# A gated linear recurrence and a gated MLP on one core: a smaller first and last unit, a different order of loads, and two decays summed on TensorE

## The chip, the cores and the metric

The kernel runs on one core of one Trainium2 chip. The metric is the device time of one execution in microseconds (us). Most executions of one kernel agree within about half a per cent. An execution that is over 1.5% above the fastest of the same kernel is called slow.

"Span" is the time from the first to the last instruction in the trace. It is about 2 us shorter than the device time of the same run.

## The reference, cut to what matters

```python
# q, k, v, a_re, a_im: (4, 8, 768, 48) float32: batch, heads, time, head size
mag = np.sqrt(a_re * a_re + a_im * a_im)
scale = np.minimum(mag, 0.999) / (mag + 1e-06)
a = a_re * scale, a_im * scale                 # complex gate, magnitude at most 0.999
for t in range(S):                             # state S: 48 x 48 for each batch and head
    S_re, S_im = a[t] * S + k[t] v[t]^T        # (complex product; k v^T is real)
    y[t] = q[t] @ S_re
x = y as (3072 tokens, 384)                    # heads side by side
g = x @ w_gate                                 # 384 x 1536
val = x @ w_val                                # 384 x 1536
ffn_out = (gelu(g) * val) @ w_out              # 1536 x 384
out = x + sigmoid(x @ w_res) * ffn_out
```

## The kernel before

The time axis is cut into 12 groups of 256 tokens (g = 0 to 11, each of C = 2 chunks of 128 tokens). Three groups make one batch element, so groups 0, 3, 6 and 9 begin with an empty state. Every other group needs the *decay* of its boundary, called M: the exponential of the log magnitudes summed over the last chunk of the group before and the first chunk of this one. The state that is carried over is multiplied by it. (The kernel before has it as a product of three factors: the last chunk of the group before, the first token of this one, and the rest of this first chunk.)

Two groups make a *unit* of 512 tokens. The program alternates two phases for each unit. `phase_x(u)` holds the output matmuls of unit u-1 (`op`), the second half of the attention of unit u, the cumulative sums of the gates (`csl`, `cst`) and the ScalarE work on the gates (Ln, Exp, Arctan, Sin). `phase_y(u)` holds the gate matmuls of unit u (`gp`, `vp`, with Gelu on ScalarE), the products q·E and k/E on VectorE, and the first half of the attention of unit u+1. All loads of `ar`, `ai` (gates), `q` and `k` are issued by SP (SyncE); those of `v` and of the weights, which also convert to bf16, by POOL (GpSimd).

The decay is a row of numbers along the free dimension, while the state wants it along the partitions. The kernel before turns it by writing the row to DRAM and reading it back, twice for each group:

```python
def turn(nm, g, srcs):
    n = len(srcs)
    md = dr.tile([n, DM], FP, tag="d" + nm, name="d" + nm)       # in DRAM
    for i, src in enumerate(srcs):
        nc.gpsimd.dma_start(out=md[i:i + 1, :], in_=src)
    m = mp.tile([128, n, H], FP, tag=nm, name=nm)
    for u in range(2):
        nc.gpsimd.dma_start(out=m[u * D:(u + 1) * D].rearrange("p r h -> p (r h)"),
                            in_=md.rearrange("r (h d) -> d (r h)", h=H))
    T[nm, g] = m

def decay0(g):                                                   # first bounce
    turn("m1", g, [T["lm", g][0:1, 0:DM]])
def decay1(g):                                                   # ScalarE
    m = T["m1", g]
    act(out=m[0:DD], in_=m[0:DD], func=AF.Exp)
def decay2(g):                                                   # second bounce
    turn("m2", g, [T["E", g - 1][127:128, DM:W], T["Ei", g][0:1, 0:DM]])
def decay3(g):                                                   # two VectorE products
    m = T["m2", g]
    M = mp.tile([128, H], FP, tag="M", name="M")
    nc.vector.tensor_tensor(out=M[0:DD], in0=m[0:DD, 0], in1=m[0:DD, 1], op=OP.mult)
    nc.vector.tensor_tensor(out=M[0:DD], in0=M[0:DD], in1=T["m1", g][0:DD, 0], op=OP.mult)
    T["M", g] = M
```

The exponential of `decay1` opens `phase_x` on ScalarE. Each engine works through its own list in order:

```python
def phase_x(u):
    g1, g2 = gs(u + 1), gs(u + 2)
    # ... cut: the lists of steps
    weave((0.0, 0.12, csls), (0.05, 0.5, zip_steps([p1(g) for g in g2])), (0.01, 0.01, dec1), (0.12, 0.45, exs),
          (0.46, 0.46, dec), (0.2, 0.65, cst), (0.7, 0.95, atn + sin), (0.95, 0.95, dec3),
          (0.0, 0.8, att), (0.1, 1.0, ops))
def phase_y(u):
    # ... cut
    weave((0.0, 1.0, gv), (0.0, 0.4, pr), (0.3, 0.95, att_steps(u + 1, 0)))

for g in gs(0) + gs(1):
    load_a(g)
for g in gs(0):
    load_q(g)                               # q, k and v
after_landing(T["k", 0], load_w_in)         # w_gate, w_val, w_res
for u in range(-1, NU + 1):
    phase_x(u)
    for g in gs(u + 3):
        load_a(g)
    if u == -1:
        for g in gs(1):
            load_q(g)
        after_landing(T["k", 2], load_w_out)
    phase_y(u)
    for g in gs(u + 3):
        load_q(g)
```

(The two numbers ahead of each list are the shares of the phase over which `weave` spreads its steps.)

Of the kernel before, what the change touches and what calls it, by code (L numbers as in the profile page):

```python
# [9 lines left out]
FP = mybir.dt.float32  # L10
BF = mybir.dt.bfloat16
AF = mybir.ActivationFunctionType
OP = mybir.AluOpType
# [15 lines left out]
def kernel(  # L29
# [23 lines left out]
    NG = B * NS  # L53
    NU = NG // 2
    MAGIC = 12582912.0
# [20 lines left out]
    ones2pi = singles.tile([128, 128], FP, name="ones2pi")  # L76
    nc.vector.memset(ones2pi, I2PI)
    mask4 = singles.tile([128, 4, 128], BF, name="mask4")
    for jm in range(4):
# [47 lines left out]
    def load_a(g):  # L127
        for nm, src in (("ar", a_re), ("ai", a_im)):
            t = lda.tile([128, C, H, D], FP, tag=nm, name=nm)
            for c in range(C):  # L130
                nc.sync.dma_start(out=t[:, c], in_=rows(src, g, c))
            T[nm, g] = t

    def load_q(g):
        for nm, src in (("q", q), ("k", k)):
            t = ldq.tile([128, C, H, D], FP, tag=nm, name=nm)
            for c in range(C):
                nc.sync.dma_start(out=t[:, c], in_=rows(src, g, c))
            T[nm, g] = t
        t = ldv.tile([128, C, H, D], BF, tag="v", name="v")  # L140
        for c in range(C):
            nc.gpsimd.dma_start(out=t[:, c], in_=rows(v, g, c))  # L142
        T["v", g] = t

    def load_w_in():

        FQ = FF // 4
        for i in range(4):
            for w, src in ((wg, moe_w_gate), (wv, moe_w_val)):
                nc.gpsimd.dma_start(out=w[:, :, i * FQ:(i + 1) * FQ],  # L150
                                    in_=src[:, i * FQ:(i + 1) * FQ].rearrange("(i p) m -> p i m", p=128))
        nc.gpsimd.dma_start(out=wr, in_=moe_w_res.rearrange("(i p) m -> p i m", p=128))
# [117 lines left out]
    def decay3(g):  # L270
# [4 lines left out]
        T["M", g] = M  # L275

    def products(g):
        def x0():
# [110 lines left out]
    def xt_step(u, jj):  # L389
        if jj == 0:  # L390
            T["xT", u] = xtp.tile([128, KD, 512], BF, tag="xT", name="xT")
        tpx = psM.tile([128, DM], BF, tag="mm", padded_shape=[128, 1024], name="tpx")
        x = T["x", u * 4 + jj]
        for f in range(KD):
# [8 lines left out]
    def gv_step(u, ffi):  # L403
        xT = T["xT", u]
        if ffi == 0:
            T["h2", u] = hb.tile([128, KF, 512], BF, tag="h2", name="h2")
        h2 = T["h2", u]
        gp = psM.tile([128, 512], FP, tag="mm", name="gp")
        for fi in range(KD):
            nc.tensor.matmul(out=gp, lhsT=wg[:, fi, ffi * 128:(ffi + 1) * 128], rhs=xT[:, fi, :],  # L410
                             start=(fi == 0), stop=(fi == KD - 1))
        vp = psM.tile([128, 512], FP, tag="mm", name="vp")
        for fi in range(KD):
# [16 lines left out]
    def op_step(u, jj):  # L430
# [6 lines left out]
        nc.vector.scalar_tensor_tensor(out=ot, in0=T["sg", u][:, jj], scalar=1.0, in1=ps, op0=OP.add, op1=OP.mult)  # L437
        nc.vector.tensor_tensor(out=ot, in0=ot, in1=T["x", u * 4 + jj], op=OP.add)
        t0 = (u * 4 + jj) * 128
        nc.sync.dma_start(out=out[t0:t0 + 128, :], in_=ot)  # L440
# [7 lines left out]
    def gs(u):  # L448
        return [2 * u, 2 * u + 1] if 0 <= u < NU else []

# [6 lines left out]
    def att_steps(u, half):  # L457

        steps = []
        for g in gs(u)[half:half + 1]:  # L460
            for c in range(C):
                steps += attention(g, c)
                if c > 0:
                    steps.insert(-1, call(xt_step, u, half * C + c - 1))
            steps.append(call(xt_step, u, half * C + C - 1))
        return steps

    def phase_x(u):

        pend = []  # L470
        g1, g2 = gs(u + 1), gs(u + 2)
        d1 = [g for g in g1 if g % NS > 0]
        d2 = [g for g in g2 if g % NS > 0]
        ops = [call(op_step, u - 1, jj) for jj in range(4)] if 0 <= u - 1 < NU else []
        att = att_steps(u, 1)
# [10 lines left out]
        def p1(g):  # L486
            return p1_steps(g) + ([call(decay0, g)] if g % NS > 0 else [])
        csls = [call(csl, g, c) for g in g1 for c in range(C)]
# [8 lines left out]
        if u < 0:  # L497

            for f in [st for g in g1 for st in p1(g)] + csls + exs + dec + zip_steps([p1(g) for g in g2]) + dec1:
                f()  # L500
            for f in atn[:1] + [call(p1_arctan, g) for g in g1] + cst + sin + atn[1:] + dec3:
                f()
            return
# [3 lines left out]
    def phase_y(u):  # L507

        gv = []
        if 0 <= u < NU:  # L510
            table("gelu_and_others")()
            gv = [call(gv_step, u, f) for f in range(KF)]
            gv = gv[:8] + [call(rp_step, u, 0), call(rp_step, u, 1)] + gv[8:] + [call(rp_step, u, 2), call(rp_step, u, 3)]
        pr = [st for g in gs(u + 1) for st in products(g)]
# [4 lines left out]
    for g in gs(0):  # L519
        load_q(g)  # L520
    after_landing(T["k", 0], load_w_in)
    for u in range(-1, NU + 1):
        phase_x(u)
        for g in gs(u + 3):
            load_a(g)
        if u == -1:
            for g in gs(1):
                load_q(g)
            after_landing(T["k", 2], load_w_out)
        phase_y(u)  # L530
        for g in gs(u + 3):
            load_q(g)


# [28 lines left out]
```

## Time and profile before

| | before |
|---|---|
| device time, median | 344.3 us (342.71 to 344.8, 4 runs) |
| span of the profiled run | 341.4 us |
| first transposes of the attention (`tp`) | 48.2 us |
| first gate matmul (`gp`) | 89.85 us |
| start of the first phase that runs at the steady pace | 120.0 us |
| a steady cycle of two phases, 512 tokens | 44.4 to 47.2 us |
| last gate phase, which no other work fills | 312.0 to 329.4 us |
| last outputs | 8.0 us |

First the span in 40 equal slices of 8.5 us, for the kernel before. A digit is the busy share in tenths. PEclk is the granted clock of TensorE, in tenths of full speed.

```profile
PE   0330544298689979899897999779999989999995
...
PEclk9996585559699999999999999999999999999999
DMA  9999999999999999527422620021000210002002
```

(The trace records the clock from 24.8 us on only; the nines before that stand for no record.) TensorE (PE) is nearly full from the twelfth slice to the end. In the first eight slices it is busy 2.6 tenths in the mean, and the next three look better than they are, since the clock is at half in the ninth and at 0.6 in the eleventh. The DMA engines are busy in every slice up to the sixteenth. So there are two limits, one after the other: the start-up, and then TensorE.

The view of windows of the kernel before says the same with numbers. Its columns are the stretch, its length, then the busy time (and number of instructions) of PE, PEld, DVE, ACT and POOL, the granted clock, the DMA share and GB/s.

```profile
100.00:130.00 30.00, 27.83 (x233) 16.93 (x235) 21.91 (x38) 22.25 (x43) 6.57 (x9) 1.00 1.12 152
...
280.00:310.00 30.00, 29.70 (x293) 18.79 (x296) 23.04 (x42) 16.81 (x31) 0.00 (x0) 1.00 0.04 15
```

The chain of waits, followed back from the last instruction, shows what the start-up is made of. These are some of its pieces in the kernel before: start, length, engine and transfer.

```profile
21.80 6.91 DMA dm_219<-ar
...
31.32 5.61 DMA m_247<-dm_244
...
44.80 13.88 DMA dm_266<-ar
...
59.62 4.62 DMA m_268<-dm_266
```

`dm` is a row on its way to DRAM and `m` the same row on its way back. A row of 384 floats is 1.5 KB. In these pieces it takes 7 to 14 us on the way out and about 5 us on the way back. The timeline of the kernel before shows who waits for it, and what the gate loads cost at the very beginning. Columns: start, length, engine, line, operation, tiles, and in brackets the idle time before it and what ended that.

```profile
10.36 4.65 SPq L131 DMA_DIRECT2D ar<-in_a_re_dram  x2
...
15.06 4.57 SPq L131 DMA_DIRECT2D ai<-in_a_im_dram  x2
...
64.32 0.21 ACT L119 ACTIVATE m_268<-m_268 96x8 f32<-96x8 f32 x1 [8.90 <-DMA m_268<-dm_266]
...
89.85 0.58 PE L410 MATMUL gp<-xT,wg 128*128 128x512 bf16 x1 [2.12 <-DVE xT L401]
```

ScalarE waits 8.9 us for a bounced row, in a phase in which TensorE waits for ScalarE. SP spends 4.6 us on a pair of gate loads of 192 KB each, because the v loads that GpSimd started are under way at the same time. That a second issuing engine gives no second path is what the Trainium skill says (DMA: Bandwidth & Descriptors, section "Issuing engines are not separate DMA queues"): all transfers interleave on the same 16 engines.

### The profile page before, as it was taken

How to read it: one execution, taken by the hardware profiler on the slowest of the kernel's cores; microseconds unless marked ns; L12 is line 12 of the kernel's file. 1: busy time of each engine (PE TensorE's matmuls, PEld its weight loads, DVE VectorE, ACT ScalarE, POOL GpSimd, SP SyncE). 2: the span in 40 equal slices, each digit the busy share in tenths (PEclk: the TensorE clock that was granted, in tenths of full speed). 3: DMA queues.
4: the chain of work that ended last, by engine and by line, in shares of the span. 5: the costliest groups of instructions: out<-in, count | busy, mean ns of one | idle time of the engine just before them, and what ended most of it. 6: DMA issues, size and time to landing. Idle time of an engine off the chain costs nothing.

```text
span 341.4 us, 5552 instructions
## 1 busy us (share of the span) xinstructions
PE 267.3 (78%) x2054; PEld 160.6 (47%) x2080; DVE 245.4 (72%) x440; ACT 203.0 (59%) x338; POOL 67.1 (20%) x104
## 2 busy tenths in 40 slices
PE   0330544298689979899897999779999989999995
PEld 0110224275256545465554566445665556565452
DVE  1322696249999649999389998499994799855443
ACT  3365434349665696756896656977568275662530
POOL 9423710050522224102232000150001300000000
PEclk9996585559699999999999999999999999999999
DMA  9999999999999999527422620021000210002002
GB/s 139 136 139 175 176 184 196 175 170 171 155 167 162 169 133 172 109 46 72 25 63 54 118 46 2 2 48 47 3 2 1 50 46 2 0 2 92 2 1 92
DMA packets 135258, 30.25 MB, mean 89 GB/s; under 512 B 127168, under 2 KB 135232, under 8 KB 135232
## 3 DMA queue, kind: packets, MB, share of 16 engines
q1 hardware_dynamic: 103296, 23.60, 40.6%
q0 software_dynamic: 31936, 6.31, 21.9%
q8 instruction: 16, 0.26, 0.3%
q14 instruction: 10, 0.08, 0.1%
HBM read 31.33 MB, written 4.76 MB: 106 GB/s over the span
## 4 chain that ended last, share of the span: by engine, by line
PE 47%; DMA 18%; DVE 15%; ACT 9%; issue 7%; POOL 3%; ACTq 0%; DVEq 0%; POOLq 0%
PE vp L414 12%; PE gp L410 11%; PE op L434 6%; DMA dm_266<-ar 4%; DMA v<-in_v_dram 4%; PE tp L320 3%; PE at L327 3%; PE tp L317 3%; PE rp L426 3%; DMA dm_663<-Ei 2%; ACT L445 2%; DVE fg L237 2%; DVE r L234 2%; DMA dm_219<-ar 2%; ACT CS L119 2%
## 5 line engine op out<-in xcount | busy, mean ns | idle before, releaser
L410 PE MATMUL gp<-xT,wg 128*128 128x512 bf16 x196 | 61.5, 382 | 7.6 <-DVE xT L401 4.6
L414 PE MATMUL vp<-xT,wv 128*128 128x512 bf16 x210 | 60.3, 382 | 0.3
L322 ACT COPY qk<-tp 96x512 bf16<-96x512 bf16 x48 | 27.9, 581 | 28.3 <-PE tp L320 15.1
L180 DVE TENSOR_TENSOR ai<-s,ai 128x768 f32<-128x768 f32 x12 | 11.1, 955 | 38.5 <-ACT s L119 26.9
L330 DVE TENSOR_TENSOR atm<-at,mask_81 128x512 bf16<-128x512 f32 x48 | 32.8, 683 | 7.2 <-PE at L327 7.2
L410 PEld LDWEIGHTS <-wg 128*128 128x128 bf16 x216 | 20.0, 98 | 23.0 <-issue 8.9
L317 PE MATMUL tp<-ident,Q 128*96 128x128 bf16 x192 | 20.1, 231 | 13.4 <-DVE qk L323 8.6
L142 POOL DMA_DIRECT2D v<-in_v_dram x24 | 21.3, 902 | 43.0 <-PE y L367 22.4
L414 PEld LDWEIGHTS <-wv 128*128 128x128 bf16 x216 | 20.4, 98 | 19.3 <-issue 0.8
L317 PEld LDWEIGHTS <-Q 128*96 128x96 bf16 x192 | 17.3, 131 | 21.4 <-issue 10.0
L323 DVE COPY qk<-tp 96x512 bf16<-96x512 bf16 x48 | 19.9, 414 | 10.1 <-ACT qk L322 9.6
L203 PE MATMUL csl<-ar,lt0a 128*128 128x384 f32 x24 | 12.3, 601 | 18.6 <-DVE ar L189 18.5
L119 ACT ACTIVATE CS<-fg,hpi 128x768 bf16<-128x768 f32 x12 | 11.2, 935 | 24.1 <-DVE fg L237 24.1
L445 ACT ACT_TABLE_LOAD x18 | 23.1, 1283 | 1.0 <-PEq L547 0.7
L320 PE MATMUL tp<-ident,K 128*96 128x128 bf16 x192 | 22.1, 235 | 0.0
L227 PE MATMUL cst<-ai,lt0b 128*128 128x384 f32 x24 | 11.6, 568 | 13.4 <-ACT ai L119 13.1
L327 PE MATMUL at<-qk 96*128 96x128 bf16 x192 | 20.4, 228 | 0.1
L437 DVE SCALAR_TENSOR_TENSOR ot<-sg,op 128x384 f32<-128x384 f32 x24 | 13.2, 549 | 9.4 <-PE op L434 9.4
L365 PE MATMUL y<-v,atm 128*128 128x48 bf16 x192 | 17.9, 187 | 2.5 <-DVE atm L330 2.4
L365 PEld LDWEIGHTS <-atm 128*128 128x128 bf16 x192 | 13.5, 98 | 12.8 <-DVE atm L330 11.6
L320 PEld LDWEIGHTS <-K 128*96 128x96 bf16 x192 | 17.3, 133 | 0.0
L357 PEld LDWEIGHTS <-K 128*96 128x96 bf16 x160 | 13.3, 138 | 6.5 <-DVE K L292 4.2
(155 smaller groups left out, 626.3 us busy)
## 6 DMA issues: line engine op xcount, KB each, us to landing
ar<-in_a_re_dram SPq DMA_DIRECT2D x24, 192.0 KB, 5.7
ai<-in_a_im_dram SPq DMA_DIRECT2D x24, 192.0 KB, 5.5
q<-in_q_dram SPq DMA_DIRECT2D x24, 192.0 KB, 5.1
k<-in_k_dram SPq DMA_DIRECT2D x24, 192.0 KB, 5.0
out_dram<-ot SPq DMA_DIRECT2D x24, 192.0 KB, 1.9
v<-in_v_dram POOLq DMA_DIRECT2D x24, 96.0 KB, 6.3
wg<-in_moe_w_gate_dram POOLq DMA_DIRECT2D x4, 288.0 KB, 9.2
wv<-in_moe_w_val_dram POOLq DMA_DIRECT2D x4, 288.0 KB, 10.5
```

The lines of the kernel that those rows point to most:

```text
L142: nc.gpsimd.dma_start(out=t[:, c], in_=rows(v, g, c))
L317: nc.tensor.transpose(out=tp[0:DD, j * 128:j * 128 + 128], in_=Q(x), identity=ident)
L320: nc.tensor.transpose(out=tp[0:DD, 512 + j * 128:640 + j * 128], in_=K(x), identity=ident)
L322: nc.scalar.copy(out=qk[0:DD, 0:512], in_=tp[0:DD, 0:512])
L323: nc.vector.tensor_copy(out=qk[0:DD, 512:1024], in_=tp[0:DD, 512:1024])
L327: nc.tensor.matmul(out=at[:, j], lhsT=qk[0:DD, 512 + j * 128:640 + j * 128], rhs=qk[0:DD, j * 128:j * 128 + 128], start=True, stop=True)
L330: nc.vector.tensor_tensor(out=atm, in0=at, in1=mask4, op=OP.mult)
L365: nc.tensor.matmul(out=ys, lhsT=st["atm", hg][:, j], rhs=V(h), start=True, stop=first)
L410: nc.tensor.matmul(out=gp, lhsT=wg[:, fi, ffi * 128:(ffi + 1) * 128], rhs=xT[:, fi, :], start=(fi == 0), stop=(fi == KD - 1))
L414: nc.tensor.matmul(out=vp, lhsT=wv[:, fi, ffi * 128:(ffi + 1) * 128], rhs=xT[:, fi, :], start=(fi == 0), stop=(fi == KD - 1))
L434: nc.tensor.matmul(out=ps, lhsT=h2[:, ffi, jj * 128:(jj + 1) * 128], rhs=wo[:, ffi, :], start=(ffi == 0), stop=(ffi == KF - 1))
L445: tab(nc.scalar.preload_act_table_set(nm))
```

## The change

Three ideas go together. (1) The loads: `v` is asked for only once the gates of the first three groups have landed, and the weights only once the gates of group 4 have. (2) The decays of groups 1 and 2 are not bounced: VectorE adds the log magnitudes of the two chunks, TensorE sums over the tokens with matmuls against a column of ones, which leaves the sum along the partitions, and ScalarE takes the exponential. (3) The units are [0], [1, 2], [3, 4], ..., [9, 10], [11]: seven instead of six. The first and the last have 256 tokens, so that the first gate matmul needs half the attention ahead of it and the last gate phase is half as long.

The diff, cut to its core (what only follows from units of two widths is left out):

```diff
-    NU = NG // 2
+    UNITS = [[0]] + [[g, g + 1] for g in range(1, NG - 1, 2)] + [[NG - 1]]
+    NU = len(UNITS)
+    NEAR = UNITS[1][-1]                                   # 2
@@
+    def sums(g):
+        ms = psM.tile([128, H], FP, tag="mm", padded_shape=[128, 512], name="ms")
+        two = pS.tile([128, W], FP, tag="s", name="two")
+        # ... cut: half(g, c) is chunk c of lm, each head's 48 columns twice
+        nc.vector.tensor_tensor(out=two.rearrange("p (h u d) -> p h u d", u=2, d=D), in0=half(g - 1, 1),
+                                in1=half(g, 0), op=OP.add)
+        for h in range(H):
+            nc.tensor.matmul(out=ms[0:DD, h:h + 1], lhsT=two[:, h * DD:(h + 1) * DD], rhs=ones1,
+                             start=(h == 0), stop=(h == H - 1), skip_group_check=True)
+        M = mp.tile([128, H], FP, tag="M", name="M")
+        act(out=M[0:DD], in_=ms[0:DD], func=AF.Exp)
+        T["M", g] = M
@@ def phase_x(u):
-        d1 = [g for g in g1 if g % NS > 0]
+        d1 = [g for g in g1 if g % NS > 0 and g > NEAR]
@@
-            return p1_steps(g) + ([call(decay0, g)] if g % NS > 0 else [])
+            return p1_steps(g) + ([call(decay0, g)] if g % NS > 0 and g > NEAR else [])
@@
         if u < 0:
-            for f in [st for g in g1 for st in p1(g)] + csls + exs + dec + zip_steps([p1(g) for g in g2]) + dec1:
+            sm = [call(sums, g) for g in range(1, NEAR + 1) if g % NS > 0]
+            for f in [st for g in g1 for st in p1(g)] + csls + exs + zip_steps([p1(g) for g in g2]) + sm:
                 f()
@@ the loads
+    after_landing(T["ai", NEAR], lambda: [load_v(g) for g in gs(0)])
+    # ... cut: SP goes on with gates, q and k
+    after_landing(T["ai", gs(2)[-1]], w_first)              # weights, v of unit 1 among them
+    after_landing(T["k", NEAR], load_w_out)
     for u in range(-1, NU + 1):
         phase_x(u)
         # ... cut
         phase_y(u)
         for g in gs(u + 3):
             load_q(g)
+            after_landing(T["k", g], call(load_v, g))
```

More of the change, by code (lines that the diff above doesn't have):

```diff
@@ L53 @@
     NG = B * NS
-    NU = NG // 2
+    UNITS = [[0]] + [[g, g + 1] for g in range(1, NG - 1, 2)] + [[NG - 1]]
+    NU = len(UNITS)
+    FIRST = UNITS[0][-1]
+    NEAR = UNITS[1][-1]
     MAGIC = 12582912.0
@@ L77 @@
     nc.vector.memset(ones2pi, I2PI)
+    ones1 = singles.tile([128, 1], FP, name="ones1")
+    nc.vector.memset(ones1, 1.0)
     mask4 = singles.tile([128, 4, 128], BF, name="mask4")
@@ L132, in load_a @@
             T[nm, g] = t
+        T["a"] = g + 1
     def load_q(g):
@@ L139, in load_q, with load_v @@
             T[nm, g] = t
+    def load_v(g):
         t = ldv.tile([128, C, H, D], BF, tag="v", name="v")
@@ L143, in load_q, with load_w_in, load_w_res @@
         T["v", g] = t
-    def load_w_in():
+    def load_w_in(i):
         FQ = FF // 4
-        for i in range(4):
-            for w, src in ((wg, moe_w_gate), (wv, moe_w_val)):
-                nc.gpsimd.dma_start(out=w[:, :, i * FQ:(i + 1) * FQ],
-                                    in_=src[:, i * FQ:(i + 1) * FQ].rearrange("(i p) m -> p i m", p=128))
+        for w, src in ((wg, moe_w_gate), (wv, moe_w_val)):
+            nc.gpsimd.dma_start(out=w[:, :, i * FQ:(i + 1) * FQ],
+                                in_=src[:, i * FQ:(i + 1) * FQ].rearrange("(i p) m -> p i m", p=128))
+    def load_w_res():
         nc.gpsimd.dma_start(out=wr, in_=moe_w_res.rearrange("(i p) m -> p i m", p=128))
@@ L274, in decay3, with half @@
         nc.vector.tensor_tensor(out=M[0:DD], in0=M[0:DD], in1=T["m1", g][0:DD, 0], op=OP.mult)
+        T["M", g] = M
+    def sums(g):
+        ms = psM.tile([128, H], FP, tag="mm", padded_shape=[128, 512], name="ms")
+        two = pS.tile([128, W], FP, tag="s", name="two")
+        def half(gg, c):
+            sl = T["lm", gg][:, c * DM:(c + 1) * DM].rearrange("p (h u d) -> p h u d", u=1, d=D)
+            return sl.to_broadcast([128, H, 2, D])
+        nc.vector.tensor_tensor(out=two.rearrange("p (h u d) -> p h u d", u=2, d=D), in0=half(g - 1, 1),
[5 more added lines that the diff above has]
+        act(out=M[0:DD], in_=ms[0:DD], func=AF.Exp)
         T["M", g] = M
@@ L390, in xt_step @@
         if jj == 0:
-            T["xT", u] = xtp.tile([128, KD, 512], BF, tag="xT", name="xT")
+            T["xT", u] = xtp.tile([128, KD, 512], BF, tag="xT", name="xT")[:, :, 0:width(u)]
         tpx = psM.tile([128, DM], BF, tag="mm", padded_shape=[128, 1024], name="tpx")
-        x = T["x", u * 4 + jj]
+        x = T["x", token(u, jj)]
         for f in range(KD):
@@ L405, in gv_step @@
         if ffi == 0:
-            T["h2", u] = hb.tile([128, KF, 512], BF, tag="h2", name="h2")
+            T["h2", u] = hb.tile([128, KF, 512], BF, tag="h2", name="h2")[:, :, 0:width(u)]
         h2 = T["h2", u]
-        gp = psM.tile([128, 512], FP, tag="mm", name="gp")
+        gp = psM.tile([128, 512], FP, tag="mm", name="gp")[:, 0:width(u)]
         for fi in range(KD):
@@ L411, in gv_step @@
                              start=(fi == 0), stop=(fi == KD - 1))
-        vp = psM.tile([128, 512], FP, tag="mm", name="vp")
+        vp = psM.tile([128, 512], FP, tag="mm", name="vp")[:, 0:width(u)]
         for fi in range(KD):
@@ L437, in op_step @@
         nc.vector.scalar_tensor_tensor(out=ot, in0=T["sg", u][:, jj], scalar=1.0, in1=ps, op0=OP.add, op1=OP.mult)
-        nc.vector.tensor_tensor(out=ot, in0=ot, in1=T["x", u * 4 + jj], op=OP.add)
-        t0 = (u * 4 + jj) * 128
+        nc.vector.tensor_tensor(out=ot, in0=ot, in1=T["x", token(u, jj)], op=OP.add)
+        t0 = token(u, jj) * 128
         nc.sync.dma_start(out=out[t0:t0 + 128, :], in_=ot)
@@ L448, in gs, with token, width @@
     def gs(u):
-        return [2 * u, 2 * u + 1] if 0 <= u < NU else []
+        return UNITS[u] if 0 <= u < NU else []
+    def token(u, jj):
+        return UNITS[u][0] * C + jj
+    def width(u):
+        return len(UNITS[u]) * C * 128
     def call(f, *a):
@@ L457, in att_steps @@
     def att_steps(u, half):
+        todo = [(g, c, i * C + c) for i, g in enumerate(gs(u)) for c in range(C)]
+        n = len(todo) // 2
         steps = []
-        for g in gs(u)[half:half + 1]:
-            for c in range(C):
-                steps += attention(g, c)
-                if c > 0:
-                    steps.insert(-1, call(xt_step, u, half * C + c - 1))
-            steps.append(call(xt_step, u, half * C + C - 1))
+        for i, (g, c, jj) in enumerate(todo[half * n:half * n + n]):
+            steps += attention(g, c)
+            if i > 0:
+                steps.insert(-1, call(xt_step, u, jj - 1))
+        if n:
+            steps.append(call(xt_step, u, half * n + n - 1))
         return steps
@@ L471, in phase_x @@
         g1, g2 = gs(u + 1), gs(u + 2)
-        d1 = [g for g in g1 if g % NS > 0]
-        d2 = [g for g in g2 if g % NS > 0]
-        ops = [call(op_step, u - 1, jj) for jj in range(4)] if 0 <= u - 1 < NU else []
+        d1 = [g for g in g1 if g % NS > 0 and g > NEAR]
+        ops = [call(op_step, u - 1, jj) for jj in range(len(gs(u - 1)) * C)]
         att = att_steps(u, 1)
@@ L497, in phase_x @@
         if u < 0:
-            for f in [st for g in g1 for st in p1(g)] + csls + exs + dec + zip_steps([p1(g) for g in g2]) + dec1:
+            sm = [call(sums, g) for g in range(1, NEAR + 1) if g % NS > 0]
+            for f in [st for g in g1 for st in p1(g)] + csls + exs + zip_steps([p1(g) for g in g2]) + sm:
                 f()
-            for f in atn[:1] + [call(p1_arctan, g) for g in g1] + cst + sin + atn[1:] + dec3:
+            for f in atn[:1] + [call(p1_arctan, g) for g in g1] + cst + sin + atn[1:]:
                 f()
@@ L512, in phase_y @@
             gv = [call(gv_step, u, f) for f in range(KF)]
-            gv = gv[:8] + [call(rp_step, u, 0), call(rp_step, u, 1)] + gv[8:] + [call(rp_step, u, 2), call(rp_step, u, 3)]
+            rp = [call(rp_step, u, jj) for jj in range(len(gs(u)) * C)]
+            gv = gv[:8] + rp[:len(rp) // 2] + gv[8:] + rp[len(rp) // 2:]
         pr = [st for g in gs(u + 1) for st in products(g)]
@@ L520, with w_first @@
         load_q(g)
-    after_landing(T["k", 0], load_w_in)
+    after_landing(T["ai", NEAR], lambda: [load_v(g) for g in gs(0)])
+    for g in gs(2):
+        load_a(g)
+    for g in gs(1):
+        load_q(g)
+    while T["a"] < 6:
+        load_a(T["a"])
+    def w_first():
+        load_w_in(0)
+        load_w_in(1)
+        load_v(gs(1)[0])
+        load_w_in(2)
+        load_w_in(3)
+        load_w_res()
+        for g in gs(1)[1:]:
+            load_v(g)
+    after_landing(T["ai", gs(2)[-1]], w_first)
+    after_landing(T["k", NEAR], load_w_out)
     for u in range(-1, NU + 1):
         phase_x(u)
-        for g in gs(u + 3):
-            load_a(g)
-        if u == -1:
-            for g in gs(1):
-                load_q(g)
-            after_landing(T["k", 2], load_w_out)
+        while u >= 0 and T["a"] < min(NG, gs(u + 1)[-1] + 6 if gs(u + 1) else NG):
+            load_a(T["a"])
         phase_y(u)
```

## The prediction

> **What bounds the kernel now.** From about 90 us TensorE does: the table of windows gives it 25.6 to 29.7 us busy in each 30 us from 100 to 310 us, at full granted clock. Before that it waits for the start-up: idle to 48 us but for 8.4 us, and the first gate matmul (gp) comes at 89.85 us (timeline). The DMA row reads 9 up to about 130 us. The chain of waits up to 90 us is mostly transfers: v loads (8.4 us) and the decay bounces through DRAM (dm_219 6.9, m_247 5.6, dm_266 13.9, m_268 4.6, dm_663 8.4, m_666 4.4 us). ScalarE sits 8.9 us (55 to 64 us) before the exponential of m_268, and TensorE 8.4 us with it. 12 v loads go out before all gates are in; beside them SP needed 4.6 us for two gate loads, at 93 to 107 us about 2.0. The Trainium skill (DMA: Bandwidth & Descriptors, "Issuing engines are not separate DMA queues") says that all queues share the same 16 engines; this trace agrees.
>
> **What the change does.**
> 1. v leaves the first 14 us. Three groups' gates (2.36 MB) at the 195 GB/s seen later land at 14 to 16 us; the first q, k, v at about 20.
> 2. The first two decays become 2 VectorE adds (0.96 us each), 16 tiny matmuls and 2 exponentials (0.2 us): about 4 us for bounces of 8 to 18. No bounce is waited for until the second large phase.
> 3. The first unit is one group: half the attention before its first gate matmul. I expect first transposes at about 35 us (48.2 before), then a ScalarE-bound phase of 27 us (54 to 89 before, less its stall), first gp at about 63 us. The weights, asked for at 30 us, are there (2.65 MB took from 37 to 57 us before).
> 4. Added: one cycle with three table loads (1.28 us each), and matmuls of 256 columns, about 110 ns each against weight loads of 98 ns, which should still hide.
> 5. The last gate phase alone on TensorE (312.8 to 329 us) halves, as do the last outputs (8 to 4 us), but this work moves into TensorE time that is already full: neutral.
>
> **Sum.** The second steady phase starts at about 82 us with one group's gate work done; before, at 120 us with two. A group costs 23 us (a cycle of two took 46.5). So 120 - 82 - 23 = 15 us, plus about 2 us of better-filled TensorE. Loads allow not much more: by 82 us about 13.5 MB must be in, at 165 GB/s.
>
> **Prediction.** 344.3 - 17 = 327 us; 8 in 10 between 315 and 338. Faster by over 2%: 0.86; within 2%: 0.11; slower: 0.03.
>
> **What would show it.** (1) The third group's gates land by 17 us; (2) no bounce and no ScalarE wait over 3 us for m1 before 64 us; (3) first gp at 58 to 69 us; (4) closing gate phase about 8 us, last outputs 4; (5) DMA still 9 to about 110 us; steady cycles still about 46 us.
>
> **What would make it wrong.** The first bounce left (group 4) stands on GpSimd's queue behind v loads that wait for late k loads; its exponential opens the second phase on ScalarE. I put it at 80 us; at 95 the gain shrinks to 5 us. Weights late for the earlier gate matmuls; the granted clock (0.50 at 50 to 76 us) staying low longer; or, on the good side, a fuller TensorE than before.

## The result, and the profile after

All ratios here are one kernel's fast runs over the fast runs of the kernel before in the same rounds on the same chip. Such a ratio is not quite the ratio of the medians that are quoted beside it. The brackets are 95% intervals.

| | before | after |
|---|---|---|
| device time, median | 344.3 us (4 runs) | 334.34 us (333.62 to 335.43, 4 runs) |
| ratio | | 0.9727 [0.969, 0.9764] |
| span of the profiled run | 341.4 us | 332.0 us |
| first transposes | 48.2 us | 39.8 us |
| first gate matmul | 89.85 us | 64.8 us |
| start of the steady phase (one group's gate matmuls done after, two before) | 120.0 us | 85.4 us |
| table loads on ScalarE | 18 | 21 |
| last gate phase | 17.4 us | 8.8 us |
| last outputs | 8.0 us | 4.1 us |

The change is faster by 10 us. The prediction was 327 us with a range of 315 to 338. The result lies inside the range, but the gain is 10 us where 17 were expected. (The chain of waits of the changed kernel goes back no further than 190 us. It shows nothing of the start, so the other views carry the comparison.)

The span in 40 slices, now of 8.3 us, of the changed kernel:

```profile
PE   0307379499876899778999798998989999899995
...
PEclk9955758789999699999999999999999999999999
DMA  8999999999999927268234193000210001100111
```

In the first eight slices TensorE is busy 4.1 tenths in the mean instead of 2.6, and the DMA row is through with its nines after 14 slices instead of 16. But there is a fresh 6 in the PEclk row at the fourteenth slice (108 to 116 us), in what should have been the first steady cycle.

The timeline of the changed kernel, on the way to that cycle:

```profile
7.14 1.97 SPq L136 DMA_DIRECT2D ar<-in_a_re_dram  x2
...
9.15 2.18 SPq L136 DMA_DIRECT2D ai<-in_a_im_dram  x2
...
13.75 0.17 POOL L171 COPY landed<-ai 1x1 f32<-1x1 f32 x1 [11.59 <-DMA ai<-in_a_im_dram]
...
24.23 5.28 PE L296 MATMUL ms<-ones,two 128*96 128x1 f32 x32 [10.29 <-DVE two L293]
...
26.99 0.17 ACT L124 ACTIVATE M<-ms 96x8 f32<-96x8 f32 x1 [5.74 <-PE ms L296]
...
29.55 0.17 ACT L124 ACTIVATE M<-ms 96x8 f32<-96x8 f32 x1 [2.39 <-PE ms L296]
29.73 1.28 ACT L470 ACT_TABLE_LOAD   x1
31.02 0.84 ACT L124 ACTIVATE ai<-ai 128x768 f32<-128x768 f32 x1
...
39.77 0.66 PE L342 MATMUL tp<-ident,Q 128*96 128x128 bf16 x4 [4.93 <-DVE Q L317]
...
64.79 0.80 PE L435 MATMUL gp<-xT,wg 128*128 128x256 bf16 x3 [4.41 <-DVE xT L426]
...
85.39 1.28 ACT L470 ACT_TABLE_LOAD   x1
86.69 0.21 ACT L124 ACTIVATE m<-m 96x8 f32<-96x8 f32 x1
```

With v out of the way a pair of gate loads takes 2.0 to 2.2 us instead of 4.6, and the third group's gates are there at 13.75 us. The sums do away with the bounces, but they have a price: ScalarE stands still for 5.74 + 2.39 = 8.1 us, because its two small exponentials stand in its list right behind the sums, ahead of the arctangents. At 86.69 us the first bounced row that is left (`m` of group 4) is used with no wait.

The wait comes 18 us later, from the *second* bounce of the same group. The timeline of the changed kernel, VectorE (DVE) and TensorE:

```profile
105.15 0.16 DVE L282 TENSOR_TENSOR M<-m 96x8 f32<-96x8 f32 x1 [1.69 <-DMA m<-dm]
105.23 0.95 DVE L317 TENSOR_TENSOR Q<-CS,qE 128x1536 bf16<-128x1536 bf16 x1
...
106.23 0.42 PE L342 MATMUL tp<-ident,Q 128*96 128x128 bf16 x4 [2.23 <-DVE Q L317]
```

The row is needed for M of group 4 only, which the attention uses some time later. But the multiply stands in VectorE's list ahead of the product `Q` of group 3, and the transposes of that `Q` are next in TensorE's own list, ahead of more gate matmuls: TensorE is idle for 2.2 us. What follows is in the windows of the changed kernel:

```profile
104.00:106.00 2.00, 0.00 (x1) 0.00 (x0) 0.85 (x2) 1.98 (x2) 0.40 (x1) 1.00 1.12 260
106.00:108.00 2.00, 1.75 (x7) 0.55 (x7) 2.00 (x5) 1.09 (x2) 0.87 (x2) 0.70 1.16 251
108.00:110.00 2.00, 1.08 (x12) 1.08 (x13) 2.00 (x3) 0.60 (x1) 0.00 (x0) 0.50 0.93 200
110.00:112.00 2.00, 2.00 (x7) 0.73 (x7) 1.53 (x4) 0.58 (x1) 0.74 (x2) 0.50 1.11 224
112.00:114.00 2.00, 2.00 (x19) 1.44 (x18) 0.74 (x2) 0.60 (x1) 1.21 (x2) 0.59 0.93 59
...
103.39:106.80 3.41, 1.18 (x8) 0.50 (x7) 1.72 (x5) 3.38 (x5) 1.20 (x2) 1.00 1.07 229
106.80:113.63 6.83, 5.89 (x31) 3.04 (x30) 5.17 (x9) 2.07 (x4) 2.02 (x4) 0.50 0.95 181
...
104.71:135.15 30.44, 27.75 (x261) 17.25 (x266) 25.39 (x45) 16.63 (x31) 5.15 (x8) 0.89 0.65 96
...
155.84:181.40 25.56, 25.34 (x260) 16.14 (x263) 23.19 (x43) 16.30 (x31) 3.02 (x3) 1.00 0.42 52
```

After the gap the granted clock falls to half, at 106.80 us, and stays there until 113.63 us. The last two lines are the same phase of two neighbouring units with the same work (260 TensorE instructions): 30.4 us in the first steady cycle, 25.6 us in the next. The first is 4.9 us longer: TensorE is busy 2.4 us longer and idle 2.5 us longer.

So the books are: the steady phase starts 34.6 us earlier (120.0 to 85.4) with one group less behind it, and a group costs 23 us, so the start has gained 11.6 us. The first cycle takes 49.75 us (85.4 to 135.15) where 46.5 are usual, which gives 3.3 back. That leaves 8.3 of the 9.4 us by which the span is shorter. What makes up the last 1.1 us is not separated.

### The profile page after: what moved, and what is told of

It reads as the page before. It is cut to its first block, busy times and chain, and to the rows that moved or that the text cites. A ratio compares the mean times of both kernels' runs of the same rounds, so it can differ in the third digit from the quotient of the medians.

```text
span 332.0 us, 5779 instructions
## 1 busy us (share of the span) xinstructions
PE 271.7 (82%) x2159; PEld 171.0 (52%) x2184; DVE 246.8 (74%) x451; ACT 209.1 (63%) x353; POOL 60.8 (18%) x100
## 2 busy tenths in 40 slices
DMA packets 134811, 30.24 MB, mean 91 GB/s; under 512 B 126720, under 2 KB 134784, under 8 KB 134784
## 5 line engine op out<-in xcount | busy, mean ns | idle before, releaser
L435 PE MATMUL gp<-xT,wg 128*128 128x512 bf16 (+1 forms) x235 | 64.4, 355 | 9.4 <-DVE xT L426 8.1
L124 ACT ACTIVATE h<-gp 128x512 bf16<-128x512 f32 (+1 forms) x84 | 44.5, 536 | 31.8 <-PE gp L435 29.7
L439 PE MATMUL vp<-xT,wv 128*128 128x512 bf16 (+1 forms) x244 | 63.1, 355 | 0.4
L442 DVE SCALAR_TENSOR_TENSOR h<-h,vp 128x512 bf16<-128x512 bf16 (+1 forms) x84 | 49.7, 603 | 11.4 <-PE vp L439 7.4
L459 PE MATMUL op<-wo,h 128*128 128x384 bf16 x288 | 50.2, 326 | 7.8 <-ACT Ei L124 5.9
L459 PEld LDWEIGHTS <-h 128*128 128x128 bf16 x288 | 27.8, 98 | 28.3 <-issue 11.0
L355 DVE TENSOR_TENSOR atm<-at,mask 128x512 bf16<-128x512 f32 x48 | 32.9, 685 | 11.4 <-PE at L352 11.3
L435 PEld LDWEIGHTS <-wg 128*128 128x128 bf16 x252 | 23.8, 99 | 23.6 <-issue 11.5
L439 PEld LDWEIGHTS <-wv 128*128 128x128 bf16 x252 | 24.1, 99 | 15.5 <-issue 0.3
L470 ACT ACT_TABLE_LOAD x21 | 26.9, 1283 | 1.1 <-PEq L595 0.7
L342 PEld LDWEIGHTS <-Q 128*96 128x96 bf16 x192 | 17.0, 130 | 15.8 <-DVE Q L317 11.6
L265 POOL DMA_DIRECT2D m<-dm x24 | 16.8, 704 | 25.3 <-DMA dm<-ar 13.2
L390 PEld LDWEIGHTS <-atm 128*128 128x128 bf16 x192 | 12.6, 97 | 13.2 <-DVE atm L355 11.9
```

The costliest lines, as they stand in the source:

```text
L124: tab(nc.scalar.activation(**kw))
L342: nc.tensor.transpose(out=tp[0:DD, j * 128:j * 128 + 128], in_=Q(x), identity=ident)
L355: nc.vector.tensor_tensor(out=atm, in0=at, in1=mask4, op=OP.mult)
L435: nc.tensor.matmul(out=gp, lhsT=wg[:, fi, ffi * 128:(ffi + 1) * 128], rhs=xT[:, fi, :], start=(fi == 0), stop=(fi == KD - 1))
L439: nc.tensor.matmul(out=vp, lhsT=wv[:, fi, ffi * 128:(ffi + 1) * 128], rhs=xT[:, fi, :], start=(fi == 0), stop=(fi == KD - 1))
L442: nc.vector.scalar_tensor_tensor(out=h2[:, ffi, :], in0=h2[:, ffi, :], scalar=0.5, in1=vp, op0=OP.mult, op1=OP.mult)
```

## The experiments

Twelve kernels were run, all with correct results. Those of one batch ran on the same chip with the kernel before beside them: 343.9 us in the first two batches, 344.0 in the third, 344.3 in the last.

### First batch: which part of the change earns the gain

**Units of two groups, all else of the change kept (label pairs).**

```diff
-    UNITS = [[0]] + [[g, g + 1] for g in range(1, NG - 1, 2)] + [[NG - 1]]
+    UNITS = [[g, g + 1] for g in range(0, NG, 2)]
```

> Undone: the units. Six units of 512 tokens as before; the new load order and the decays summed on TensorE stay (groups 1 and 2). Theory (the gain is the time at which the second large phase starts, and loads and sums alone move it too): first gate matmul at about 75 us, second phase at about 104 us against 120 before, total about 331 us, so as good as the change itself or within 3 us of it. Rival (the small first and last units earn the gain): 340 us or more.

Measured: fast runs 332.06 to 332.85 us, ratio 0.9667 [0.9617, 0.9716]. The profiled run was a slow one (380 us) and is left aside. The six units of before, with the new loads and sums, are at least as fast as the seven of the change. So the small units, as the change has them, do not earn the 10 us. (The loads are tied to the units, so they move a little too: in six units v waits for the gates of four groups instead of three, and the weights for those of group 5 instead of 4. The same holds for the other two kernels of six units below.)

**The sums undone: all decays bounced again (bounce).**

```diff
-        d1 = [g for g in g1 if g % NS > 0 and g > NEAR]
+        d1 = [g for g in g1 if g % NS > 0]
-            return p1_steps(g) + ([call(decay0, g)] if g % NS > 0 and g > NEAR else [])
+            return p1_steps(g) + ([call(decay0, g)] if g % NS > 0 else [])
-            sm = [call(sums, g) for g in range(1, NEAR + 1) if g % NS > 0]
+            sm = []
```

> Undone: the sums on TensorE; the decays of groups 1 and 2 go through DRAM again, units and load order stay. Theory: their second bounce is issued at about 55 us behind the weights and lands at 66 to 72 us, VectorE waits for it in order, the first steady phase (85 us in the change) starts 4 to 8 us later, total 338 to 342 us. Rival (the bounces were not on the path once v is out of the way): within 1.5 us of the change, 334 us.

Measured: 344.64 us, ratio 1.003 [0.9982, 1.0077]. The whole gain is gone, more than expected. Without the sums the first transposes come at 31.4 us (39.8 in the change) and the first gate matmul at 56.7 (64.8): the price of the sums is about 8 us there. But then VectorE waits, as the timeline of this kernel shows:

```profile
75.48 0.16 DVE L282 TENSOR_TENSOR M<-m 96x8 f32<-96x8 f32 x1 [18.02 <-DMA m<-dm]
```

An 18 us wait for one bounced row moves the steady phase to 98.4 us, 13 us later than in the change. The direction was expected, the size was not: 4 to 8 us. The last of the rows was sent off at 57.46 us, after GpSimd had issued the weights (from 29.7 to 51.9 us), and its way to DRAM alone kept GpSimd waiting for 11.9 us. So this run prices the bounces beside the new load order, and not the bounces alone.

**The old order of the v loads (early_v).**

```diff
-    after_landing(T["ai", NEAR], lambda: [load_v(g) for g in gs(0)])
+    for g in gs(0) + gs(1) + gs(2):
+        load_v(g)
     # and no v load behind the weights or behind the k of these groups
```

> Undone: the late v. The v loads of groups 0 to 4 go out first as before; units, sums and late weights stay. Theory: the third group's gates land at about 21 us instead of 13.75, and the start moves by 4 to 6 us, but the ten v loads are then not in the way at 30 to 75 us, so 1 to 3 us come back: total 336 to 339 us. Rival (the sum of bytes decides, not their order): no change, 334 us.

Measured: 339.94 us, ratio 0.989 [0.9836, 0.9944]. The first transposes move to 46.6 us and the steady phase to 92.9. The timeline of this kernel has the slow pairs of gate loads back:

```profile
10.34 4.64 SPq L136 DMA_DIRECT2D ar<-in_a_re_dram  x2
```

So the order of the loads is worth about 5.6 us (339.94 less 334.34), and the sums about 10. Together that is more than the 10 us of the whole, so the two do not simply add up: with either of them undone the start is held up.

**A small first unit, but a pair at the end (pair_last).**

```diff
-    UNITS = [[0]] + [[g, g + 1] for g in range(1, NG - 1, 2)] + [[NG - 1]]
+    UNITS = [[0]] + [[g, g + 1] for g in range(1, NG - 3, 2)] + [[NG - 3], [NG - 2, NG - 1]]
```

> Undone: the small last unit alone. Units of 256 tokens are the first and the one before the last pair; the last is of 512. Same start, same number of units. Theory (the work of the last unit only moves into TensorE time that is full anyway): within 2 us of the change, 334 to 336 us. Rival (the short last gate phase, 8 instead of 16 us alone on TensorE, earns about 8 us): 340 us or more.

Measured: 337.84 us, ratio 0.9816 [0.9761, 0.9871]. It falls between the two expectations, and its interval just touches that of the change. The start is nearly the same (86.2 us, 85.4 in the change). The windows of this kernel, and then of the change, from the start of the fourth unit's phase to the end:

```profile
182.78:336.50 153.72, 140.94 (x1093) 84.73 (x1091) 114.17 (x210) 90.66 (x157) 15.06 (x24) 1.00 0.13 31
```

```profile
181.40:332.00 150.60, 138.28 (x1078) 84.52 (x1091) 113.54 (x210) 90.88 (x157) 15.21 (x24) 1.00 0.14 32
```

The same groups take 3.1 us longer with the pair at the end. So the small last unit does earn about 3 us, where the prediction had called it neutral. At what place of those 150 us they are earned stays open. A small unit is moved here rather than removed, so this run does not price the seventh unit as such.

### Second batch: the waits of the start

**The sums later in the start (late_exp).** TensorE sums behind the `cst` matmuls, VectorE copies the result out, and the exponential waits for the next Exp table.

```diff
-        act(out=M[0:DD], in_=ms[0:DD], func=AF.Exp)           # in sums(g)
+        nc.vector.tensor_copy(out=M[0:DD], in_=ms[0:DD])
         T["M", g] = M
+
+    def mexp(g):
+        M = T["M", g]
+        act(out=M[0:DD], in_=M[0:DD], func=AF.Exp)
@@ phase_x
-        dec1 = [call(decay1, g) for g in d1]
+        dec1 = [call(decay1, g) for g in d1] + [call(mexp, g) for g in g1 if g % NS > 0 and g not in d1]
@@ first phase
-            for f in ... + zip_steps([p1(g) for g in g2]) + sm:
+            for f in ... + zip_steps([p1(g) for g in g2]):
-            for f in atn[:1] + [call(p1_arctan, g) for g in g1] + cst + sin + atn[1:]:
+            for f in atn[:1] + [call(p1_arctan, g) for g in g1] + cst + sm + sin + atn[1:]:
```

> Only the place of the sums moves: the two sums are formed after the first angles' matmuls, kept in SBUF, and their exponentials are taken at the start of the next phase, so ScalarE need not wait 8.1 us for TensorE at 21 to 30 us. Theory (a second chain binds next: the bounce of group 4, whose m1 is ready at about 85 us): first transposes at 31 to 32 us instead of 39.8, first gate matmul at about 57 instead of 64.8, but the first steady phase still starts at 83 to 86 us; total 332 to 335 us, at most 2 us gained. Rival (only the start-up chain counts): 8 us gained, 326 us.

Measured: 335.69 us, ratio 0.9767 [0.9708, 0.9827], no better than the change. The start is 4.7 us faster (transposes at 35.1 us, gate matmuls at 60.1, steady phase at 80.7): the transposes and gate matmuls come some 3 us later than expected, the steady phase at least 2 us earlier, and the total lies just above the expected range. All of the gain is given back in the phase behind. The timeline of this kernel, and its window of that phase:

```profile
108.22 0.16 DVE L282 TENSOR_TENSOR M<-m 96x8 f32<-96x8 f32 x1 [6.82 <-DMA m<-dm]
...
109.31 0.66 PE L346 MATMUL tp<-ident,Q 128*96 128x128 bf16 x4 [7.36 <-DVE Q L321]
```

```profile
102.66:137.82 35.16, 27.55 (x261) 17.18 (x266) 25.39 (x45) 16.62 (x30) 7.16 (x11) 0.85 0.66 97
```

The row of group 4 does not come earlier with the earlier start: VectorE has it at 105.15 us in the change and at 108.22 here. The phase begins 2.05 us earlier (102.66 instead of 104.71) and the row comes 3.07 us later; together that is the longer wait, 6.8 us instead of 1.7. Why the row comes later was not looked into. The expectation had put this wait on ScalarE, at the first bounce. It is on VectorE, at the second one, with TensorE idle for 7.4 us behind it and at half clock from 105.6 to 115.8 us.

**Group 4's decay summed on TensorE too (sum4), both together (late_both), and both in six units (pairs_late).** The sum of the next unit's groups is asked for inside the phase before (cut: the bounce of group 4 goes, and in sum4 too its sum is copied out by VectorE and its exponential taken in the phase that needs it):

```diff
+        sm = [call(sums, g) for g in g2 if g % NS > 0 and g in SUMMED]     # SUMMED: groups 1 to 4
-              (0.46, 0.46, dec), (0.2, 0.65, cst), ...
+              (0.46, 0.46, dec), (0.6, 0.6, sm), (0.2, 0.65, cst), ...
```

> Only group 4's decay is moved to TensorE as well, its exponential taken at the start of the phase that needs it; groups 1 and 2 stay as in the change. Theory: m1 of group 4 was ready just in time at 86.7 us, so the phase starts at 85 as before; gone are VectorE's wait of 1.7 us for the second bounce at 105 us, TensorE's idle 2.2 us there and the half clock from 106 to 113 us: 2 to 5 us gained, 329 to 332 us. Rival (the half clock comes from something else): under 1 us gained.

> Both together. Theory (two chains in parallel, each hides the other): the first steady phase starts at about 77 us, the gain is larger than the sum of the two alone: 10 to 12 us, 322 to 325 us. Rival (loads bind next, with the DMA engines busy to 110 us): 328 us or more.

> Both together in the six units of 512 tokens (sums for groups 1, 2, 4 and 5). Theory (units of 256 earn nothing at the start and the cycle more costs a few us; six units measured 2 us less than the change): 322 to 326 us, level with the same edits in the change's units. Rival (the small units pay off once the start-up chain is short): 3 us or more slower than those.

Measured, medians of the fast runs: sum4 337.77 us (three fast runs, 337.63 to 340.02, and a slow one), 0.9853 [0.9785, 0.9922]; late_both 333.66 us (four fast runs), 0.971 [0.9651, 0.9769] (its profiled run was slow, so its trace is not used); pairs_late 332.71 us, 0.9685 [0.9637, 0.9734]. All three lie 6 to 9 us above the upper end of what was expected; only that pairs_late is about level with late_both came out. The reason is in the edit, as the view of waits of sum4 shows (who, for whom: us in total, times, longest):

```profile
PE ms L296 <- DVE two L293: 6.5, 1, 6.5
```

The sum needs a VectorE addition, which stands behind other work in VectorE's list. TensorE takes its own list in order too, so it stood 6.5 us at the first of these matmuls with other work behind it, and ScalarE 6.7 us behind TensorE. In pairs_late the same wait was 6.0 us. For late_both it is argued from the equal code only. One wait had been taken away and another put in, so these runs do not test the theory.

### Third batch: the wait for the second bounce taken away

**late_exp, and the two multiplies moved to where M is used (late_dec3).** For the second group of a unit they now come at 0.35 of `phase_y`, behind the products of the first group.

```diff
-        dec3 = [call(decay3, g) for g in d1]
+        dec3 = [call(decay3, g) for g in d1 if g == g1[0]]
@@ phase_y
-        weave((0.0, 1.0, gv), (0.0, 0.4, pr), (0.3, 0.95, att_steps(u + 1, 0)))
+        d3 = [call(decay3, g) for g in gs(u + 1)[1:] if g % NS > 0 and g > NEAR]
+        weave((0.0, 1.0, gv), (0.0, 0.4, pr), (0.35, 0.35, d3), (0.3, 0.95, att_steps(u + 1, 0)))
```

> The kernel of the late exponentials (335.7 us; its start is 4.7 us earlier, but VectorE then waits 6.8 us at 101 to 108 us for group 4's second bounce and TensorE idles 7.4 us) with one more move: the two multiplications that take that bounce up are emitted a third of the way into the next phase, for groups that stand second in their unit and need it only a phase later. Theory (an in-order VectorE wait on the second bounce gave the start's gain back): the wait and the idle time are gone, 5 to 7 us gained on that kernel, 328.5 to 331 us. Rival (what VectorE waited for only hides the loads behind it): 334 us or more.

Measured: 329.08 us (327.62 to 329.88), ratio 0.9566 [0.9505, 0.9627], as expected, and 6.6 us below late_exp on the same chip. The transfer is not a bit faster. The multiply now comes after it, as the timeline and then the window of the same phase show for this kernel:

```profile
113.91 0.16 DVE L282 TENSOR_TENSOR M<-m 96x8 f32<-96x8 f32 x1
```

```profile
103.92:130.55 26.63, 24.55 (x259) 16.04 (x261) 24.00 (x44) 16.67 (x31) 5.33 (x8) 1.00 0.82 117
```

There is no idle time before the multiply, and the phase takes 26.6 us instead of 35.2, with the clock at 1.00.

**No bounce at all in the first three units (units_best), and the same in six units of two (pairs_best).** The sums of groups 1 and 2 stand behind `cst`, and ScalarE takes their exponentials at the start of the next phase, straight from PSUM, where TensorE left the sums. Group 4 is summed at the start of the phase before its use, where VectorE has its inputs ready.

```diff
+    SUMMED = [g for u in UNITS[:3] for g in u]
@@ start of phase_x
+        near = [g for g in range(1, NEAR + 1) if g % NS > 0] if u == 0 else []
+        far = [g for g in g1 if g % NS > 0 and g in SUMMED and g > NEAR]
+        weave((0.0, 0.0, [call(sums, g) for g in far]), (0.0, 0.0, [call(mexp, g) for g in near]),
+              (0.02, 0.02, [call(mexp, g) for g in far]), (0.0, 0.12, csls), ...
```

> The change's units with no bounce before the third phase: sums of groups 1 and 2 after the first angles' matmuls, exponentials straight from PSUM at the start of the next phase; group 4 summed at the start of the phase before its use, when its inputs have long been ready (the earlier try waited 6.5 us on TensorE for them). Theory: first transposes at about 32 us, first gate matmul at about 57, first steady phase at 77 to 80, total 323 to 327 us. Rival (loads bind, as the DMA engines are busy to 110 us): 330 us or more, with waits for ai or k loads in the first steady phase.

> The same in six units of 512 tokens (sums for groups 1, 2, 4 and 5). Theory (small units earn nothing, a cycle less is saved): 321 to 327 us, within 2 us of the same edits in the change's units. Rival: 3 us or more slower.

Measured: units_best 326.63 us (325.71 to 327.08), ratio 0.9505 [0.9455, 0.9555]; pairs_best 329.55 us (328.66 to 331.17), ratio 0.9599 [0.9543, 0.9655]. The timeline and the window of units_best:

```profile
31.76 0.66 PE L345 MATMUL tp<-ident,Q 128*96 128x128 bf16 x4 [0.42 <-DVE Q L320]
...
56.69 0.80 PE L438 MATMUL gp<-xT,wg 128*128 128x256 bf16 x3 [4.39 <-DVE xT L429]
```

```profile
102.17:128.20 26.03, 23.96 (x259) 15.96 (x261) 23.61 (x42) 16.63 (x30) 5.19 (x8) 1.00 0.94 142
```

The transposes start as early as with no sums at all (31.8 us against 31.4 in bounce), and the phase takes its ordinary time. This version beats both kernels: the kernel before by 17.4 us, the change by 7.7 us (medians; the change was timed in other rounds; its ratio is 0.9727 against 0.9505). The two had been expected within 2 us of each other. The six units were 2.9 us slower, no run of the one overlapping with the other. So the small units do earn some 3 us once no wait at the start takes them away. That is the size which pair_last shows for the last unit alone. If the last unit is worth 3 us in the change too, as pair_last says, the first one cost some 5 us there (3.1, and the 2.2 us by which pairs' fast median of 332.15 lies below the change) and about nothing in units_best: an estimate, since no run has the small first unit undone alone. In the change the small units together earned nothing beside pairs; that the wait for group 4 had eaten it up is argued from these numbers, since the trace of pairs is a slow one and can't be used.

### Last run: the change with only the multiplies moved

**dec3_only** is the change itself with the two-line edit of late_dec3 and nothing else.

> The change with one move only: the two VectorE multiplications that take up the second bounce are emitted a third of the way into the next phase for groups that stand second in their unit. The start stays (transposes at 39.8, second phase at 85 us). Theory: gone is VectorE's wait of 1.7 us at 103 to 105 us, with TensorE's 2.2 us of idle time, and the half clock that followed from 106 to 113 us, which I put at 3.3 us: 3 to 6 us gained on the change, 328.5 to 331.5 us. Rival (only the wait itself counts, the half clock costs nothing): 1.5 to 2.5 us gained, 332 to 333 us.

Measured over 5 rounds: 331.5 us (330.66 to 332.86, 6 runs), ratio 0.9616 [0.9577, 0.9655], the upper end of what was expected. The interval lies wholly below that of the change, 0.9727 [0.969, 0.9764]. The medians are 2.8 us apart; the difference of the ratios, 0.0111, is 3.8 us of 344. VectorE's `Q` and multiply in this kernel, and its window of the phase:

```profile
105.60 0.95 DVE L317 TENSOR_TENSOR Q<-CS,qE 128x1536 bf16<-128x1536 bf16 x1
...
116.92 0.15 DVE L282 TENSOR_TENSOR M<-m 96x8 f32<-96x8 f32 x1
```

```profile
106.93:133.56 26.63, 24.78 (x263) 16.03 (x261) 24.00 (x44) 16.66 (x30) 6.13 (x8) 1.00 0.75 104
```

26.6 us instead of 30.4, so the multiply's place in VectorE's list costs the change 3.8 us in this phase. Its wait was only 1.7 us.

Of the 3.8 us the two profiled runs keep 2.4, since the start did not stay in this one: the steady phase begins at 87.61 us instead of 85.39, with the same code up to there. That later start did not take the wait away by itself. The row came later too: its last leg was issued from 104.05 us and took about 4 us, so `Q` would have waited for it. And pair_last, which starts 0.8 us later than the change with the multiply in its old place, waits 2.2 us.

In the phase TensorE is busy 24.8 us instead of 27.75, at clock 1.00 instead of 0.89, for the same matmuls. These 3.0 us agree with the 6.83 us at half clock seen after the gap. They are not isolated from the gap itself: the three traces with the gap (the change, pair_last, late_exp) all have the half clock behind it.

## Why the prediction was right or wrong

- **What bounds the kernel** ("Before that it waits for the start-up"; from about 90 us "TensorE does"): right. The runs with a trace that can be used, pair_last apart, moved with the start of the steady phase or with its first cycle. (One reading is off: TensorE was busy for 12.3 us before 48 us, not 8.4. Nothing later rests on it.)
- **Step 1, "Three groups' gates ... land at 14 to 16 us"**: right, 13.75 us. early_v shows the cause: with the old order the pairs of loads take 4.6 us again and 5.6 us of the gain are lost.
- **Step 2, "16 tiny matmuls and 2 exponentials (0.2 us): about 4 us for bounces of 8 to 18"**: the mechanism was right (bounce loses the whole gain), the size was not. The sums kept TensorE for 5.3 us and ScalarE waiting for 8.1 us. The cost that was missing is that of order: an exponential of 0.17 us held up the arctangents behind it. The first transposes came at 39.8 us instead of "about 35". units_best shows that it was the place and not the work: the same sums behind `cst` leave the transposes at 31.8 us.
- **"No bounce is waited for until the second large phase"**: right in the letter. The first wait for a bounce was in that phase.
- **Step 3, "first gp at about 63 us"**: right, 64.8 us, and "the second steady phase starts at about 82 us": 85.4.
- **Step 4, three more table loads**: 21 instead of 18, at 1283 ns each. They were no visible loss.
- **Step 5, "neutral"** for the smaller last unit: the view was right (8.8 and 4.1 us), the value wrong. pair_last puts it at about 3 us, in the good direction.
- **"steady cycles still about 46 us"**: wrong for the first cycle, and this is the step that failed. It took 49.75 us. The prediction had named the right group (4) and the right queue, but the wrong one of its two bounces: it feared "its exponential opens the second phase on ScalarE". That exponential did not wait. The second row did, on VectorE, 1.7 us, with 2.2 us of idle TensorE and 6.8 us at half clock behind it. late_exp, where the wait grew with an earlier start and a later row, and late_dec3 and dec3_only, where it went while the bounce stayed, settle this.
- **"plus about 2 us of better-filled TensorE"**: not seen separately.

In numbers: of the 17 us expected, 15 were for the earlier start. That was worth 11.6 (3.4 us lost; late_exp, with the exponentials out of the way, starts its steady phase at 80.7 us), and the first cycle gave back 3.3. The two terms together are most of the 7 us between 327 and 334. units_best takes both away and lands at 326.6 us. That it meets the predicted figure is partly chance, since it also has no bounce for group 4.

## What to carry to other kernels

A small operation that waits for a transfer costs what stands behind it in its engine's list. So put it at its first use, not where its other inputs are ready; a two-line move of this kind was worth about 3 us here, and nothing had to become faster. When a change brings a phase forward, look for the next transfer that the phase will now meet early: an earlier start can turn into a longer wait one phase on. And when a part of a change seems to earn nothing, try it again once the wait behind it is gone: the two small units together were worth 3 us only then.

## What the Trainium skill lacked or had wrong

- TensorE: Matmul & The Clock Gate, section "What's actually happening", has the half clock set in after at least one idle window of about 3.4 us and end after a busy one. It also says that the windows run freely, so that they need not begin where a gap begins. The traces agree with windows of 3.413 us: the half clock lasted 6.83 us in the change and 10.24 us in late_exp, two and three of them, and in both the last one had TensorE busy throughout. What the page lacks is how idle a window has to be. In the change the window ahead of the half clock (103.39 to 106.80 us) had TensorE busy for 1.18 us around a gap of 2.2 us. In dec3_only the two windows from 104.52 to 111.35 us, busy for 2.12 and 2.48 us, kept clock 1.00. In between, busy time alone does not tell: 1.70 us (kernel before, 82.87 to 86.29 us) led to the half clock, 1.65 us (units_best, 92.77 to 96.18 us) did not.
- ScalarE: Activation LUTs, section "What ACT_TABLE_LOAD costs", gives about 1283 ns and another 1380 ns of drain for every switch. The 1283 ns agree (mean of 18 and of 21 loads). The drain is not in these traces: at 29.7 us in the change the last exponential ends at 29.72 us, the load starts at 29.73 and the next function at 31.02, which is 1.30 us in all. Wherever the next function follows with no other wait, it starts at most 0.11 us behind the load.
- DMA: Bandwidth & Descriptors, "Specifications", puts line rate at 512 B and more. This kernel's rows are 192 B (126,720 of 134,811 packets are under 512 B), and with the engines 90% busy or more the slices of the changed kernel moved 134 to 212 GB/s; no run here has longer rows to compare. The page has no trn2 rate for such rows on loads that SP issues: here SP was through with a pair of 192 KB in 2.0 to 2.2 us with no v loads beside them and in 4.6 us with them.
- The same page fits one transfer as 2 us plus its size. Rows of 1.5 KB bounced through DRAM took 4.6 to 13.9 us each way here while the engines were full, and one such bounce kept VectorE waiting for 18 us. A figure for a whole small transfer beside full engines is missing.
- None of its pages prices a sum over partitions with one-column fp32 matmuls: 16 of them, in 32 records, took 5.3 us at a granted clock of about 0.5.
